# An attention and mixture-of-experts kernel: score and attention tiles of one PSUM bank, value columns in two parts, and the last gate logits summed ahead

## The chip, the cores and the metric

One Trainium2 chip, of which the kernel uses one core. A core has five engines, each with its own queue, worked off in order: TensorE (PE, matrix products; its weight loads are listed apart as PEld), VectorE (DVE), ScalarE (ACT), GpSimd (POOL) and SyncE (SP, which here only issues transfers). The 16 DMA engines move the data. PE writes its results to PSUM, eight banks of 512 floats on each of 128 partitions, and DVE and ACT read them there. Engines wait for each other on semaphores. The metric is the device time of one execution in microseconds (us); lower is better.

## What is computed

Causal attention with a window of 128 positions and a linear bias for each head, and behind it a mixture of experts in which every token goes to one expert, and every expert keeps at most 80 tokens, those of the largest gate weight. Batch 8, 8 heads, 576 positions, head size 64; 4608 tokens of 512 numbers; 8 experts with an inner size of 1024. All inputs are float32.

```python
scores = scale * np.matmul(q, k.transpose(0, 1, 3, 2))
bias = slopes[:, None, None] * (-np.abs(rel).astype(np.float32))[None, :, :]
mask = (rel >= 0) & (rel < window)
scores = np.where(mask, scores + bias[None], -1000000000.0)
attn = np.exp(scores - np.max(scores, axis=-1, keepdims=True))
attn = attn / (np.sum(attn, axis=-1, keepdims=True) + 1e-09)
x = np.matmul(attn, v)            # then tokens x 512
...
logits = x @ w_gate
expert_idx = np.argmax(logits, axis=1)
logits_shift = logits - logits.max(-1, keepdims=True)
probs = np.exp(logits_shift)
probs /= probs.sum(-1, keepdims=True) + 1e-09
gate_w = probs[np.arange(N), expert_idx]
...
for e in range(E):
    tok_idx = np.where(expert_idx == e)[0]
    if len(tok_idx) > capacity:
        tok_idx = tok_idx[np.argpartition(-gate_w[tok_idx], capacity)[:capacity]]
    h = np.maximum(x[tok_idx] @ w1[e], 0.0)
    out[tok_idx] = gate_w[tok_idx, None] * (h @ w2[e])
```

## The kernel before

**Recording.** The program isn't issued as it is written. A layer, `Plan`, records every instruction, orders them by its own table of costs and by the dependences between tiles, and then issues each engine's list. So nearly every row of the trace names line 352, where the layer issues, and rows are told apart by tiles. A dependence is kept per tile: an instruction that overwrites a tile waits for all that read the tile before.

**Units and steps.** The attention is cut into 144 units, 18 to a batch. A unit `i` is two halves (`hh` 0 and 1, the two heads that share a 128-row tile of `q` and `kp`). `scores(i)` makes four matmuls (the trace lists every float32 product of these kinds twice, so eight) into `sps[i % 2]`, a tile of two PSUM banks, a bank for each half; DVE adds the bias and takes the row's extremum (`e`, `mn`), POOL or ACT scales. `turned(i)` transposes `e` on PE into `pt`, ACT takes the exponential into `ptb`. `attend(i)` makes twelve matmuls (24 in the trace) of `ptb` with the values `v` into `avp`, again one tile of two banks, alternating between the halves in pairs. After every sixth unit `attended(n)` copies `av` to `xs` on ACT. The main loop runs over steps `c` of two units; nine steps `r` = 0 to 8 make a batch. At step `c` the scores of units 2c+4 and 2c+5 stand beside the attend of units 2c-2 and 2c-1.

**Gate logits and value columns.** The gate needs the logits of each attention output, which is a weighted sum of values. So the values are multiplied by the gate weights first: `value_logits(b)` multiplies the transposed values `l_vt` with `wg` (four groups by two banks, 16 in the trace) into the spare columns of a score tile, DVE or ACT adds a one and writes `lxb`; `value_columns(b)` transposes `lxb` back (five transposes, into both banks) and eight DVE copies lay the results into columns 64 to 72 of the value tile `v`. The attend matmuls then give output, logits and the sum of the exponentials together. For batch b+1 this stands at r = 3 and r = 8 of batch b; for batch 0 ahead of the loop, in the av banks, with copies aside into `xs`.

**Selection.** The choice of an expert and of the kept tokens of each batch (`merge_steps`) is spread over the steps of the batches behind it: `front` (norm, `gate`, parts) at r = 0 to 2, `turn` at 4, `diffs` at 5 to 7, `places` and `keep` at 0 and 1 of the next, `put_kept` at 2. For the last batch all of it stands behind the attention. There PE is kept busy with 100 small matmuls (`keep_clock`), which the layer places where PE would idle; ten larger ones (`warm_up`) stand ahead of the experts. Then tokens are gathered, eight experts are worked off, and the results are scattered.

**Transfers.** SP issues all loads and stores, in order, on eight rotating semaphores. `transfers(c)` names up to three for each step: the next batch's `l_vt`, `v`, `k`, `q`, the stores of the batch before (`store_x`). Where it has `None`, a filling transfer is taken from the list `fill` (pieces of the first two experts' weights, and zero writes of the output); what is left goes out behind the attention. At the start SP's order is: keys and queries of pair 0 in two pieces each, four `l_vt`, two small transfers of the gate weights (64x4x8), pair 1, four `v`, pairs 2 and 3.

## Time and profile before

| what | value |
|---|---|
| runs (us) | 338.27, 337.01, 338.03; median 338.03 |
| profiled execution (us) | 338.06 |
| its span (us) | 336.0 |
| mean granted clock of TensorE | 0.979 of full |
| PE, PEld busy | 92%, 67% |
| DVE, ACT, POOL busy | 56%, 43%, 39% |

The span is what the profiler sees from the first instruction to the last; the execution's own time is 2.06 us longer. All times of rows count from the start of the span. A row of a timeline gives start, duration, engine, line, operation, the tile written and the tile read, the shape and the count of merged instructions, and in brackets how long the engine had been idle and who released it. The granted clock is a share of the full 2.4 GHz.

### The profile page before, as it was taken

Reading aid. Unit: us, or ns where it says so; the run is one execution under the profiler, and the core shown is the slowest. Engines: PE = TensorE matmul, PEld = TensorE weight load, DVE = VectorE, ACT = ScalarE, POOL = GpSimd, SP = SyncE. Lnnn points to the kernel's source line nnn. Section 1 sums busy time; section 2 is a strip of 40 time slices with the busy share of each in tenths; the row PEclk is TensorE's granted clock in tenths of the full one; section 3 lists DMA queues with packets and bytes.
Section 4 is the critical chain, followed back from the end, with each engine's and each line's share of the span. In section 5 each row is a group of like instructions: output and inputs, shape, how many; then the busy total and the mean of one; then the engine's idle time right before and its main releaser. Section 6 shows DMA issues by size and latency. Waiting matters only on the chain. (4 is left out here: it accounts for less than half of the span.)

```text
span 336.0 us, 16380 instructions
## 1 busy us (share of the span) xinstructions
PE 309.5 (92%) x6722; PEld 223.8 (67%) x6722; DVE 188.2 (56%) x1017; ACT 145.1 (43%) x351; POOL 129.6 (39%) x350
## 2 busy tenths in 40 slices
PE   7897988989989989998998998999789999999993
PEld 6365755677777777776777777878585576655660
DVE  8854584787778678678678768777511011110100
ACT  1462664546555555454554554661213222233221
POOL 7443464428437336444644743830071111011111
PEclk9699999999999999999999999999789999999999
DMA  7969998899989998998998988778159999999930
GB/s 199 376 203 286 353 289 280 256 306 305 335 281 276 297 303 283 299 294 242 333 320 262 313 295 301 288 273 301 45 157 295 387 393 397 401 397 395 397 108 26
DMA packets 45530, 97.01 MB, mean 289 GB/s; under 512 B 5392, under 2 KB 5904, under 8 KB 45456
## 3 DMA queue, kind: packets, MB, share of 16 engines
q1 hardware_dynamic: 44432, 93.17, 81.4%
q0 software_dynamic: 1024, 2.81, 2.9%
q8 instruction: 53, 0.87, 1.2%
q14 instruction: 21, 0.17, 0.2%
HBM read 74.14 MB, written 21.81 MB: 286 GB/s over the span
## 5 line engine op out<-in xcount | busy, mean ns | idle before, releaser
L352 POOL TENSOR_SCALAR e<-e,mn 128x192 f32<-128x192 f32 (+1 forms) x216 | 88.7, 419 | 97.7 <-DVE mn L352 85.6
L352 ACT ACTIVATE ptb<-pt 128x256 f32<-128x256 f32 (+1 forms) x144 | 61.8, 463 | 58.3 <-PE pt L352 58.1
L352 PE MATMUL s<-kp,q 64*64 64x192 f32 (+1 forms) x1152 | 77.1, 319 | 10.3 <-DVE v L352 6.2
L352 PE MATMUL av<-v,ptb 64*64 64x73 f32 x3072 | 83.3, 228 | 2.4 <-issue 1.1
L352 PEld LDWEIGHTS av<-v,ptb 64*64 64x64 f32 x3072 | 71.2, 132 | 16.7 <-issue 12.1
L352 DVE CUSTOM_DVE_ANT_0 e<-s,bneg 128x192 f32<-128x192 f32 x192 | 60.6, 352 | 29.6 <-PE s L352 19.4
L352 PE MATMUL pt<-ident,e 128*128 128x128 f32 x400 | 60.6, 285 | 0.9 <-issue 0.4
L352 PEld LDWEIGHTS pt<-ident,e 128*128 128x128 f32 x400 | 43.2, 142 | 12.0 <-issue 4.4
L352 PEld LDWEIGHTS s<-kp,q 64*64 64x64 f32 x1152 | 36.7, 133 | 15.0 <-DVE v L352 7.2
L1297 DVE TENSOR_TENSOR ys<-ys,y 80x512 f32<-80x512 f32 x8 | 5.5, 683 | 73.4 <-ACT ys L1292 73.4
L352 ACT ACTIVATE e<-e,mn 128x192 f32<-128x192 f32 (+1 forms) x72 | 31.8, 441 | 31.9 <-DVE mn L352 31.9
L1290 PE MATMUL y<-w,hT 128*32 128x512 f32 (+1 forms) x288 | 42.8, 594 | 0.0
L1265 PEld LDWEIGHTS h<-xgTs,w 128*64 128x64 f32 x1024 | 35.9, 137 | 6.5 <-issue 6.0
L1265 PE MATMUL h<-xgTs,w 128*64 128x80 f32 x1024 | 37.2, 233 | 0.3 <-ACT xgTs L1224 0.3
L1241 POOL DMA_INDIRECT out_dram<-ys,sid x8 | 7.4, 922 | 72.0 <-ACT hT L1270 66.8
L352 ACT COPY xs<-av 128x438 f32<-128x438 f32 (+3 forms) x57 | 26.5, 509 | 14.4 <-PE av L352 13.5
L1290 PEld LDWEIGHTS y<-w,hT 128*32 128x32 f32 (+1 forms) x288 | 10.5, 105 | 25.0 <-issue 24.2
L352 DVE TENSOR_SCALAR_CACHE_REDUCE ncm<-s 128x272 bf16<-128x272 f32 (+8 forms) x69 | 22.7, 380 | 2.1 <-ACT ncm L352 1.6
L352 DVE DVE_READ_ACCUMULATOR2_ANT mn<- 128x1 f32 x288 | 23.8, 83 | 0.0
L352 DVE CUSTOM_DVE_ANT_0 e<-s,bn 128x128 f32<-128x128 f32 x64 | 16.0, 288 | 9.8 <-PE s L352 6.9
L1270 ACT ACTIVATE hT<-h 128x320 f32<-128x320 f32 x16 | 7.0, 437 | 29.1 <-PE h L1265 29.1
L352 DVE CUSTOM_DVE_ANT_0 e<-s,bnx 128x192 f32<-128x192 f32 x32 | 10.2, 355 | 16.3 <-PE s L352 16.2
(147 smaller groups left out, 326.9 us busy)
## 6 DMA issues: line engine op xcount, KB each, us to landing
w<-in_moe_w_dram SPq DMA_DIRECT2D x48, 512.0 KB, 11.1
v<-in_v_dram SPq DMA_DIRECT2D x32, 328.5 KB, 5.0
x_dram<-xs SPq DMA_DIRECT2D x32, 292.0 KB, 4.7
l_vt<-in_vt_dram SPq DMA_DIRECT2D x32, 288.0 KB, 4.4
out_dram<-zero SPq DMA_DIRECT2D x36, 256.0 KB, 3.8
kp<-in_k_dram SPq DMA_DIRECT2D x31, 288.0 KB, 4.9
q<-in_q_dram SPq DMA_DIRECT2D x31, 288.0 KB, 4.5
w<-in_moe_w_dram SPq DMA_DIRECT2D x32, 256.0 KB, 4.5
```

The costliest lines, as they stand in the source:

```text
L352: c.ins = c.f(*c.args, **c.kw)
L1241: put = nc.gpsimd.indirect_dma_start(out=out, out_offset=bass.IndirectOffsetOnAxis(ap=sid[:, e:e + 1], axis=0), in_=ys, in_offset=None, bo ...
L1265: nc.tensor.matmul(hp[64 * hh:64 * hh + 64, R * fi:R * fi + R], lhsT=a[:, cc, f0:f0 + 64], rhs=xgT[:, cc], start=(cc == 0), stop=(cc == NC ...
L1270: relu = nc.scalar.activation(hT[:, 4 * f2:4 * f2 + 4].rearrange("p c r -> p (c r)"), hp[:, 0:4 * R], AF.Relu)
L1290: nc.tensor.matmul(o, lhsT=hT[:, f_, l0:l1], rhs=c[:, f_], start=st, stop=sp)
L1297: nc.vector.tensor_tensor(ys, ys, yp[0:R, 0:DM], ALU.add)
```

## The change

A tile for each PSUM bank: `sps` is two by two tiles and `avp` two, so each wait is for one bank. `attended` copies by half, so the copies at n = 1 are six instead of three; in the last batch the second half of the last copy is on DVE. `value_columns` works in two parts: units 0 to 2 into the first bank at r = 8, with four copies, and units 3 and 4 into the second bank at r = 2 of the batch itself, with four copies. For batch 0 the logits of groups 0 and 1 come first, with copies straight from `av`; groups 2 and 3 follow at c = 1 and 2, and the logits of batch 1 move from r = 3 to r = 6. The gate weights come as one transfer of 128x128, laid out on the host. The last batch's logits are summed in three parts (`logit_sum`), two of them in the loop. A few copies of the selection go to ACT, the last batch's stores of units 3 and 4 are issued earlier, and `transfers` has four `None` instead of six a batch.

```diff
-    sps = [psum.tile([P, 2, 512], F32, name=f"s{i}") for i in range(2)]
-    avp = psum.tile([P, 2, 512], F32, name="av")
+    sps = [[psum.tile([P, 512], F32, name=f"s{i}_{k}") for k in range(2)] for i in range(2)]
+    avp = [psum.tile([P, 512], F32, name=f"av{k}") for k in range(2)]
...
     load_pair(0, 0)
-    for g in range(NP):
+    wg = const.tile([P, NP, 32], F32, name="wg")
+    nc.sync.dma_start(out=wg.rearrange("p g c -> p (g c)"), in_=w_gate)
+    for g in range(2):
         load_vt(0, g)
-    wg = const.tile([P, NP, 32], F32, name="wg")
-    nc.gpsimd.memset(wg, 0.0)
-    for hh in range(2):
-        nc.sync.dma_start(
-            out=wg[64 * hh:64 * hh + 64, :, 9 * hh:9 * hh + 8],
-            in_=w_gate.rearrange("(g hh p) e -> hh p g e", g=NP, hh=2)[hh],
-        )
     load_pair(0, 1)
-    for g in range(NP):
+    for g in range(2):
         load_v(0, g)
+    for g in range(2, NP):
+        load_vt(0, g)
     load_pair(0, 2)
     load_pair(0, 3)
+    for g in range(2, NP):
+        load_v(0, g)
...
-        nc.vector.tensor_copy(ttt[b % 2][:, S:S + R], kp[0:KS, 0:R])
+        (nc.scalar.copy if b == LAST else nc.vector.tensor_copy)(ttt[b % 2][:, S:S + R], kp[0:KS, 0:R])
...
+    def lay(b, bank, gs, us, hh, par):
+        rows, of = (LOW, HIGH)[hh], (LOW, HIGH)[par]
+        u0, u1 = us
+        lv = bank[:, 0:32 * (gs[1] - gs[0]) * (u1 - u0)].rearrange("p (u g c) -> p g u c", u=u1 - u0, c=32)
+        k1 = min(2 * u1, NKB)
+        nc.vector.tensor_copy(
+            vts[b % 2][rows, gs[0]:gs[1], 2 * u0 + par:k1:2, D:VW],
+            lv[of, :, 0:(k1 - 2 * u0 - par + 1) // 2, 9 * hh:9 * hh + 9])
+
+    def value_columns(b, bank, us, gs=(0, NP)):
+        lx, ch = lxs[b], slice(32 * gs[0], 32 * gs[1])
+        n = ch.stop - ch.start
         with nc.together():
...
+        for hh in range(2):
+            for par in range(2):
+                lay(b, bank, gs, us, hh, par)
...
     def attended(n):
...
+        for hh in range(2):
+            copy = nc.vector.tensor_copy if hh and b == LAST and n == 2 else nc.scalar.copy
+            av = avp[hh][:, 0:6 * VW].rearrange("p (s c) -> p s c", c=VW)
+            if n == 1:
+                copy(xs[:, 3].rearrange("p (g h) c -> p h g c", h=2)[:, hh], av[:, 0:4])
+                for j, rows in ((0, LOW), (1, HIGH)):
+                    copy(
+                        xs[0:64, 4].rearrange("p (u j h) c -> p j h u c", u=2, j=2)[:, j, hh], av[rows, 4:6])
...
+    def logit_sum(b, n=None):
+        whole_, first, last = (0, NU, 0, H), n == 0, n == 2
+        u0, u1, h0, h1 = {None: whole_, 0: (0, 3, 0, 4), 1: (3, NU, 0, H), 2: (0, 3, 4, H)}[n]
+        U, N = u1 - u0, h1 - h0
+        ve = nc.vector if last else nc.gpsimd
...
+        ve.tensor_tensor(
+            lw, xs[:, :, :, D:VW - 1], xs[:, :, :, VW - 1:VW].broadcast_to([P, U, N, E]), ALU.mult)
+        to = small.tile([P, U, E], F32, tag="lg2", name=f"lg2_{b}", bufs=1) if last else lg
+        nc.vector.tensor_reduce(to, lw.rearrange("p u h e -> p u e h"), axis=AX.X, op=ALU.add)
+        if last:
+            nc.vector.tensor_tensor(lg, lg, to, ALU.add)
...
-        if b < LAST and r == 3:
+        if b < LAST and r == (3 if b else 6):
             yield value_logits(b + 1, two, add_ones)
         if b < LAST and r == 8:
-            yield value_columns(b + 1, two)
+            yield value_columns(b + 1, two[0], (0, 3))
+        if b and r == 2:
+            yield value_columns(b, two[1], (3, NU))
+        if c == 1:
+            yield value_logits(0, two, add_ones, (2, NP))
+        if c == 2:
+            yield value_columns(0, two[0], (0, NU), (2, NP))
...
-            3: v_[3:4] + x_[1:2] + [None],
+            3: v_[3:4] + x_[1:2],
...
-            7: kq(3) + [None],
+            7: kq(3),
             8: vt_[0:1] + [None, None],
         }[r]
-        if b == 0 and r < 4:
-            at_ = [[], vt_[0:2], vt_[2:4] + v_[0:1], v_[1:4]][r]
+        if b == 0 and r < 8:
+            at_ = {
+                2: vt_[0:1], 3: vt_[1:4], 4: kq(0) + v_[0:1], 5: v_[1:4], 6: kq(1) + kq(2)[0:1],
+                7: kq(2)[1:2] + kq(3),
+            }.get(r, [])
...
-    whole(value_logits(0, (avp[:, 0], avp[:, 1]), add_ones_act))
+    whole(value_logits(0, avp, add_ones_act, (0, 2)))
     make_bias(1)
     scored(3)
+    whole(value_columns(0, avp[0], (0, NU), (0, 2)))
     strict(turned, 2)
     scored(4)
-    whole(value_columns(0, (avp[:, 0], avp[:, 1]), xsb[1].rearrange("p u h c -> p (u h c)")[:, 0:NU * P]))
...
+        if b == LAST and r in (3, 6):
+            logit_sum(b, r // 3 - 1)
...
-    while fill:
+    for _ in range(8):
         fill.pop(0)()
     keep_clock(nc.last, 100)
...
-    for u in range(NU):
+    for u in range(3):
         store_x(LAST, u)
+    while fill:
+        fill.pop(0)()
```

The order of the instructions shows the places where this acts. The first is PE at step r = 8 of batch 2, where the value columns of batch 3 are made (`lxb_317` of before is `lxb_320` of the changed kernel; brackets name the engines and transfer queues that an instruction waits for). Before:

```order
L352 MATMUL av_83<-v0_94,ptb51_342 64x73 x6
L352 MATMUL s1_82<-kp1_91,q3_1_331 64x128 [waits DMAHW2_49,DMAHW1_49,DVE_49]
L352 MATMUL s1_82<-kp1_91,q3_1_331 64x128 x3
L352 MATMUL s1_82<-ident_102,lxb_317 128x128 x4
L352 MATMUL s1_82<-ident_102,lxb_317 64x128
```

The same place of the changed kernel:

```order
L352 MATMUL s1_0_83<-kp1_94,q3_1_334 64x128 [waits DMAHW7_49,DMAHW0_49,DVE_49]
L352 MATMUL s1_0_83<-kp1_94,q3_1_334 64x128
L352 MATMUL s1_1_84<-kp1_94,q3_1_334 64x128 [waits DVE_49]
L352 MATMUL s1_1_84<-kp1_94,q3_1_334 64x128
L352 MATMUL s1_0_83<-ident_105,lxb_320 128x128 x3
```

The first bank takes three transposes, and the second half of the scores has a wait of its own; the other two transposes stand some 125 rows later, at r = 2 of batch 3.

The second place is ACT at the end of a batch's second group, n = 1, in batch 1. Before:

```order
L352 ACTIVATE ptb31_258<-pt1_80 128x384 [waits PE_49,Activation_49]
L352 COPY xs1_123<-av_83 128x2x4x73 [waits PE_49]
L352 COPY xs1_123<-av_83 64x2x2x73 x2
L352 ACTIVATE e35_262<-e35_262,mn35_263 128x3x64 [waits DVE_49,Activation_49,Pool_49]
L352 ACTIVATE ptb32_264<-pt0_79 128x384 [waits PE_49,Activation_49]
```

The same in batch 3 of the changed kernel:

```order
L352 ACTIVATE ptb67_415<-pt1_80 128x384 [waits PE_49,Activation_49]
L352 COPY xs1_126<-av0_85 128x4x73 [waits DMAHW1_49,PE_49]
L352 COPY xs1_126<-av0_85 64x2x73 [waits DMAHW4_49]
L352 COPY xs1_126<-av0_85 64x2x73
L352 COPY xs1_126<-av1_86 128x4x73 [waits PE_49]
L352 COPY xs1_126<-av1_86 64x2x73 x2
L352 ACTIVATE e71_419<-e71_419,mn71_420 128x3x64 [waits DVE_49,Activation_49,Pool_49]
```

Three copies of both banks became three of the first bank and three of the second.

The third place is DVE at the start, where the reduction of unit 3 (`e3`) and the columns of batch 0 stand. Before:

```order
L352 SCALAR_TENSOR_TENSOR bnx_89<-rp_86 64x192 x4
L352 CAST pf_159<-pi_158 128x1 [waits Pool_49]
...
L352 CAST ita_120<-ij_164 80x640 [waits Pool_49]
L352 ISA e3_137,mn3_138<-s1_82,bn0_88 128x2x64 [waits PE_49]
...
L352 COPY xs1_123<-av_83 128x128 [waits Activation_49]
L352 COPY xs1_123<-av_83 64x128
L352 COPY v0_94<-xs1_123 64x2x5x9 [waits DMAHW5_49,DMAHW4_49,DVE_49]
```

The changed kernel:

```order
L352 SCALAR_TENSOR_TENSOR bnx_92<-rp_89 64x192 x3
L352 ISA e3_140,mn3_141<-s1_0_83,bn0_91 128x2x64 [waits DVE_49,PE_49]
...
L352 TENSOR_SCALAR ts0_109<-pf_162 128x5 [waits DVE_49]
L352 ISA e4_143,mn4_144<-s0_0_81,bneg_90 128x3x64 [waits PE_49]
...
L352 COPY v0_97<-av0_85 64x2x5x9 [waits DMAHW1_49,DMAHW2_49,PE_49,Activation_49]
L352 COPY v0_97<-av0_85 64x2x4x9
```

The reduction of unit 3 moved ahead of the constants, and the copies aside are gone.

## Rows read from the trace of the kernel before

**Rows 1.** The page, busy time, share of the span and instructions of each engine.
```profile
PE 309.5 (92%) x6722; PEld 223.8 (67%) x6722; DVE 188.2 (56%) x1017; ACT 145.1 (43%) x351; POOL 129.6 (39%) x350
```

**Rows 2.** Busy time by stretch: length, PE, PEld, DVE, ACT, POOL, clock, DMA share, GB/s.
```profile
8.00:15.00 7.00, 5.78 (x40) 2.60 (x40) 6.04 (x36) 2.79 (x7) 3.38 (x14) 0.51 1.04 364
...
20.00:34.40 14.40, 12.15 (x336) 8.87 (x328) 6.01 (x36) 6.39 (x16) 5.06 (x13) 1.00 0.89 277
...
116.30:143.30 27.00, 25.69 (x648) 19.77 (x642) 20.68 (x120) 14.25 (x36) 13.63 (x36) 1.00 0.92 298
...
236.40:248.30 11.90, 8.73 (x66) 7.21 (x64) 5.12 (x24) 1.74 (x7) 4.54 (x6) 0.71 0.17 44
248.30:326.60 78.30, 78.30 (x1404) 48.62 (x1408) 9.23 (x14) 22.26 (x45) 10.32 (x12) 1.00 0.96 349
```

**Rows 3.** Waits of PE, 36 to 222 us: total, times, longest.
```profile
PE s L352 <- DVE v L352: 6.2, 7, 0.9
```

**Rows 4.** Timeline, r = 8 of batch 3, all engines.
```profile
123.08 2.02 DVE L352 COPY v<-s 64x108 f32<-64x108 f32 x8
...
123.71 0.56 PE L352 MATMUL av<-v,ptb 64*64 64x73 f32 x24
124.34 0.95 ACT L352 COPY xs<-av 128x438 f32<-128x438 f32 x2 [0.44 <-PE av L352]
...
125.15 0.56 PE L352 MATMUL s<-kp,q 64*64 64x192 f32 x8 [0.88 <-DVE v L352]
```

**Rows 5.** Timeline, r = 2 of batch 4, PE and, apart, DVE.
```profile
133.02 0.51 PE L352 MATMUL s<-kp,q 64*64 64x192 f32 x8
...
135.40 0.36 DVE L352 CUSTOM_DVE_ANT_0 e<-s,bnx 128x192 f32<-128x192 f32 x1 [1.17 <-PE s L352]
```

**Rows 6.** Timeline, n = 1 copies of batch 4, all engines.
```profile
143.34 1.35 ACT L352 COPY xs<-av 128x584 f32<-128x584 f32 x3 [1.07 <-PE av L352]
...
143.94 0.77 PE L352 MATMUL pt<-ident,e 128*128 128x128 f32 x5
...
144.75 0.26 PEld L352 LDWEIGHTS av<-v,ptb 64*64 64x64 f32 x9 [0.28 <-ACT xs L352]
```

**Rows 7.** Groups of ACT by shape: count, busy, mean ns, idle before.
```profile
L352 ACT COPY xs<-av 64x292 f32<-64x292 f32 x16 | 6.4, 399 | 0.1
...
L352 ACT COPY xs<-av 128x584 f32<-128x584 f32 x8 | 5.2, 651 | 5.9 <-PE av L352 5.9
```

**Rows 8.** Groups of DVE by shape, the value columns' copies.
```profile
L352 DVE COPY v<-s 64x108 f32<-64x108 f32 x28 | 7.5, 268 | 0.3
...
L352 DVE COPY v<-s 64x72 f32<-64x72 f32 x14 | 3.2, 225 | 0.2
...
L352 DVE COPY v<-s 64x36 f32<-64x36 f32 x14 | 2.8, 198 | 0.2
```

**Rows 9.** Timeline, the start.
```profile
10.78 2.15 PE L352 MATMUL av<-l_vt,wg 128*32 128x288 f32 x16 [0.88 <-DMA wg<-in_moe_w_gate_dram]
...
13.63 0.29 DVE L352 CUSTOM_DVE_ANT_0 e<-s,bn 128x128 f32<-128x128 f32 x1
...
17.14 0.47 PE L352 MATMUL av<-v,ptb 64*64 64x73 f32 x7 [0.66 <-ACT v L352]
...
26.54 1.16 PE L352 MATMUL s<-l_vt,wg 128*32 128x288 f32 x10 [1.66 <-DMA l_vt<-in_vt_dram]
...
29.43 0.56 PE L352 MATMUL s<-kp,q 64*64 64x192 f32 x8 [0.59 <-DVE lxb L352]
```

**Rows 10.** Timeline, behind the attention.
```profile
228.76 0.56 DVE L352 TENSOR_TENSOR ob<-tt,itb 128x400 bf16<-128x400 f32 x1
...
231.00 3.97 PE L352 MATMUL pt<-identb 128*128 128x128 bf16 x68
...
232.50 0.20 DVE L352 TENSOR_REDUCE mx<-lg 128x5 f32<-128x40 f32 x1
...
237.75 0.31 DVE L352 TENSOR_SCALAR_CACHE_REDUCE ncm<-s 128x144 bf16<-128x144 f32 x1 [1.60 <-ACT ncm L352]
```

More of the change, by code (lines that the diff above doesn't have):

```diff
@@ L811, in gate @@
         ve = nc.vector if b in FAST else nc.gpsimd
[L812 to L817 removed]
+        if b < LAST:
+            logit_sum(b)
+        lg = sums[b]
         mx = small.tile([P, NU], F32, tag="mx", name=f"mx{b}")
```

110 lines of the change are left out of this document (46 added, 64 removed).

## The prediction

> **What bounds the kernel now.** I read the page's busy shares first, then the table of busy time by stretch, the waits of PE, and the timelines around each wait. PE is busy 309.5 of 336.0 us and no other engine comes near [rows 1], so an edit is worth what it gives back to PE: idle time of PE, or time in which its clock is low. By stretch [rows 2]: a batch in the middle (116.3 to 143.3 us, one of seven periods alike) has 25.69 us of PE work in 27.0, so 1.3 us are idle. The stretch of the experts, 248.3 to 326.6, is PE without a gap at the full clock; the change leaves its instructions as they are, so nothing is won there. Two stretches show the granted clock at or near the lower of its two levels, 1.2 GHz for 2.4: 8 to 15 us (0.51) and, in part, 236.4 to 248.3 (0.71). Both are chains of waits, as is the first attention up to 34.4 us, with 12.15 us of PE work in 14.4.
>
> The idle time of the batches has one main name: over 36 to 222 us PE waits 7 times, 6.2 us in all, for DVE's copies of the value columns [rows 3]. The profiled execution took 338.06 us, 2.06 more than its span; the median of the three runs is 338.03, so the sum below is made against 338.06 and needs no correction.
>
> **The change part by part.**
>
> *Value columns in two parts, banks apart (batches 1 to 7).* Before, five transposes fill both banks of one score tile and eight copies empty them: DVE is on them from 123.08 to 125.10, while PE, done with its av matmuls at 123.71 + 0.56 = 124.27, waits until 125.15 to write the next scores there, 0.88 idle [rows 4]. Now three transposes go into the first bank at this place, with four copies, and the other two with four smaller copies follow some three steps later, in the second bank. Four large copies of 268 ns overlap: eight took 2.02, or 0.25 each, so I count 1.05. Begun at 123.08 they end at 124.13, and 0.14 before PE wants the bank. The second bank is free from the start. So the wait goes: 7 x 0.88 = **-6.2**. It is a tight cover: if the four start 0.35 later, 7 x 0.2 = 1.4 comes back.
>
> The second part lands where DVE has idle time: soon after the third step's small copies it waits 1.17 us for PE [rows 5], and the four copies are two of 225 and two of 198 ns [rows 8], some 0.75 overlapped. They stand ahead of a score reduction that feeds PE through POOL and ACT, so I charge 0.1 a batch, **+0.7** in 7 batches; bounds 0 (the idle time takes all) and 0.4 each, half of the 0.75.
>
> *Copies by half after attention.* At the end of a batch's second group ACT makes three copies in 1.35 us, and PE, after its transposes, waits 0.28 to overwrite av [rows 6]. Now there are six. The short form costs 399 ns at 292 elements and the long one 651 at 584 [rows 7], so 0.86 ns an element and some 0.15 fixed; a copy of 128x292 is 0.40, of 64x146 0.27, six together 2 x 0.40 + 4 x 0.27 = 1.88, less five overlaps of 0.05 (three rows summing to 1.45 took 1.35) = 1.63. The second bank is thus free 0.28 later than now, and PE, whose attend matmuls alternate between banks in pairs, gets only two matmuls ahead. 8 x 0.28 = **+2.2**, the 8 from [rows 7]; bounds 0 (ACT starts on the first bank earlier and PE's transposes last longer) and +3.5 (0.44 each). The other copies keep their number and now wait for one bank each: nothing.
>
> A rule of the Trainium skill (Perfetto Trace Analysis, Optimizing Scalar/DVE Operations) speaks against the split: every ScalarE or VectorE instruction has a fixed cost, put at about 51 ns for ScalarE on PSUM, and grouping pays if the engine is saturated. By that figure three more copies are 0.15 us, an estimate, 1.2 in 8 batches, and the sum below would end 1.0 lower. The fixed part read from the rows is about three times as large, and the rows decide here.
>
> *The waits themselves.* A tile per bank gives each unit's second half of scores a semaphore wait of its own: the order shows 113 more waits among PE's score groups and 20 more among its attends. A group that has such a wait and finds it satisfied starts without a gap: the scores at 133.02 have no idle time in front [rows 5]. I take 0; the upper bound is a rival below.
>
> Steady part: -6.2 + 0.5 + 2.2, **-3.3**; bounds -6.2 and, with every upper end, +1.5.
>
> *The start.* PE waits until 10.78 for the second of two small gate transfers that stand behind four value loads; its 16 logit matmuls then take 2.15 at half clock, and the chain runs over scores (DVE at 13.63), ACT's copies aside, and copies back, to the first attend at 17.14, itself 0.66 late [rows 9]. Now the gate weights are one transfer ahead of the value loads, groups 0 and 1 alone (8 matmuls, half of 2.15) go first, and DVE copies straight from PSUM; in DVE's order the reduction of unit 3 moves from behind fourteen small constants to ahead of them. 0.88 + 1.07 = 1.95 less before unit 3: the first attend at about 15.2, **-1.9**. Bounds -0.9 (only the wait for the gate weights goes, DVE holds the rest) and -2.5.
> The other half of the logits comes back behind it: 8 matmuls at the full clock and five transposes, 0.95 us of PE (16 in 2.15 at half clock make 8 in 0.54 at the full one; five transposes of twice the columns took 0.77 [rows 6], so 0.4): **+0.95**.
> Batch 1's logits: before, PE stood 1.66 for a value transfer and 0.59 for what DVE made of it [rows 9]. The change moves these logits three steps later, behind transfers that are issued only a step later: 2.25 go, and ten matmuls that took 1.16 run at the pace of data already there, some 0.5 less: **-2.7**, bounds -1.7 (the DVE wait stays) and -2.8. New waits for eight more DVE instructions among the first units, 0.1 each at half of them: **+0.45**, bounds 0 and 1.5.
> The new order of transfers brings pair 1 of keys and queries forward and costs 48 KB more of gate weights, 0.2 us of the transfers' time at 224 GB/s or more [rows 2], ahead of nothing that is late now. Start: **-3.2**, bounds -0.2 and -4.4.
>
> *The tail.* Before, DVE reaches the maximum of the last logits at 232.50, after a product and a sum over 320 elements; most of that is now made two steps ahead, and only 96 elements are left, behind DVE's own copy of the second half of av. From the end of ob, 228.76 + 0.56 = 229.32, I count that copy at 0.55, as ACT's (two in 0.95 [rows 4]) and a little more, and five short operations at 0.2 to 0.25 each (the maximum over 40 elements takes 0.20 [rows 10]): the maximum at about 231.0, 1.5 earlier. The sums ahead run on POOL and DVE in the last batch, where both have idle time. But PE's filler (68 matmuls, 3.97 from 231.00 [rows 10]) stands in the queue before the next transposes; 58 of them take 3.39 and end 0.58 earlier. So PE's queue is next late: **-0.6**. Then DVE's first reduction of the pairwise comparison, which waited 1.60 until ACT had done another bank at 237.75 [rows 10], waits only for PE, 0.65 earlier: **-0.65**, bounds 0 (ACT's part ends last) and -0.7. Two more small norms fall among DVE's work for batch 6: **+0.15**.
> Tail: **-1.1**, bounds 0 and -1.5.
>
> *Transfers.* The filling ones are only spread otherwise, in SP's queue as before; the last weights are needed after 248.3. Eight of the zero writes stay ahead of the stores of x and three go behind. Cost nothing where the cover is the 0.17 DMA share of 236.4 to 248.3 [rows 2]; without it, 3 x 256 KB at the 349 GB/s of the next row is 2.2 us more before the gathers.
>
> Sum: -3.3 - 3.2 - 1.1 = -7.6, so 338.06 - 7.6 = 330.46, **330.5 us**.
>
> **The rivals.**
> *A second stall in the place of the first.* The four copies come late, the six copies cost their upper bound and the second part its own: 1.4 + 1.3 + 2.1 = 4.8 of the gain is lost, 335.3. For it speaks the cover of only 0.14; against it that the score reduction which now stands ahead reads the second bank first. With half of it, 332.9.
> *More than counted.* The split copies cost nothing, since PE goes on with the first bank, and the start reaches its bound: -5.5 - 4.4 - 1.1 = -11.0, thus 327.1.
> *The start gives nothing.* DMA share is 0.89 from 20 to 34.4 us [rows 2], and batch 1's keys are now issued behind hoisted zero writes; a stall like the old one, 1.66 and 0.59, returns at keys and queries, and the start is worth -0.95: 332.7.
> *The waits cost (the other side).* Each of the 133 additional waits of PE delays the queue. From 57 ns each (7.6 / 133), about one filler matmul (3.97 / 68 = 58), the whole gain is gone; at 80 ns the time is 341.1. Against it stands the gapless row at 133.02; for it only that no row of before has two such waits within one unit's scores.
> *The change does not do what it says*: the copies still block both banks. The order speaks against it, since each bank has its own wait.
>
> **How the numbers follow.** The forecast with its own range 328.5 to 332.5: 0.53. A second stall: 0.15. More than counted: 0.12. The start gives nothing: 0.10. The waits cost: 0.06. No effect of the banks: 0.04. The range 326.5 to 335.5 holds the first four but for the ends of the second and third. Half a per cent, 1.7 us, is about what a measurement of this kernel can tell from no change, so faster is under 336.4: the first four cases, some of the last two; 0.88. Within: 0.07. Slower: 0.05.
>
> **What would show it.** Right: no PE wait for DVE's value copies at the last step of a batch; PE's wait for ACT before the third group's attend grown from 0.28 to about 0.56; periods of batches near 26.5; the first attend near 15.2; no wait for the value transfer of batch 1; the maximum near 231.0 less what was gained ahead of it, with the filler ending last; DVE's comparison released by PE. Wrong: idle time of 0.05 or more in front of the second half of many score groups, a new DVE wait in each batch's third step, or PE idle after 20 us for keys.

## The result

The changed kernel took 333.5 us, the median of four runs (332.67 to 338.03), beside 338.1 us for the kernel before (337.01 to 338.27). The ratio is 0.9862, with a 95% interval of 0.9828 to 0.9897: 1.4% faster, 4.6 us of the 7.6 that the prediction counted. Medians in this document are over all executions, ratios leave those out that the chip disturbed, and since the profiles of after_again, slots_again, shift_128, same_again and warm_15 are of such executions, the sizes of their waits are told but no cause rests on them.

The profiled execution took 333.14 us with a span of 331.4. From its page: span, busy time by engine, TensorE's granted clock in 40 slices (tenths, 9 is 90% or more), and the queue that carries instructions (packets, MB, share).

```profile
span 331.4 us, 16415 instructions
...
PE 308.1 (93%) x6727; PEld 224.7 (68%) x6727; DVE 192.4 (58%) x1026; ACT 146.5 (44%) x372; POOL 129.8 (39%) x351
...
PEclk9999999999999999999999999999779999999998
...
q8 instruction: 53, 0.87, 1.0%
```

PE is busy 1.4 us less than in [rows 1] and the span is 4.6 shorter, so 3.2 us of the gain is idle time that went. Where, three stretches tell, cut at ACT's n = 1 copies of batch 0 and of batch 7 and at the first expert's products (length, then busy time of PE, PEld, DVE, ACT, POOL, clock, DMA share, GB/s). Changed kernel:

```profile
30.95:217.53 186.58, 178.46 (x4467) 137.21 (x4459) 144.49 (x815) 102.80 (x274) 94.17 (x254) 1.00 0.92 305
217.53:241.59 24.06, 20.86 (x347) 17.70 (x339) 14.61 (x73) 7.55 (x25) 6.22 (x10) 0.93 0.46 154
241.59:331.40 89.81, 83.62 (x1436) 51.15 (x1436) 9.78 (x15) 23.98 (x48) 11.27 (x13) 0.96 0.84 308
```

The same stretches of the kernel before:

```profile
34.40:222.53 188.13, 177.58 (x4450) 136.09 (x4443) 141.50 (x812) 100.20 (x252) 95.32 (x255) 1.00 0.91 297
222.53:248.29 25.76, 22.14 (x347) 18.59 (x339) 14.46 (x73) 7.28 (x20) 5.79 (x9) 0.87 0.49 167
248.29:336.00 87.71, 81.97 (x1436) 49.49 (x1436) 9.92 (x15) 24.01 (x48) 11.29 (x13) 1.00 0.87 316
```

So the start gave 34.40 - 30.95 = 3.45, the seven periods 188.13 - 186.58 = 1.55, the tail 25.76 - 24.06 = 1.70, and the experts took 89.81 - 87.71 = 2.10 back. 3.45 + 1.55 + 1.70 - 2.10 = 4.60, the difference of the spans.

**The periods.** Waits of PE in the first of these stretches of the changed kernel (total, times, longest; waits under 0.15 us aren't counted):

```profile
PE s L352 <- issue: 4.5, 8, 1.1
PE av L352 <- issue: 2.1, 5, 0.6
PE av L352 <- ACT xs L352: 0.7, 4, 0.2
PE pt L352 <- issue: 0.4, 1, 0.4
```

DVE's value copies are gone from the list: 6.2 us in seven waits [rows 3]. ACT costs 0.7, after 0.5. New is the sum of the waits put down to "issue", in which PE waits for nothing that the profile shows: 7.0 us here, 3.5 in the kernel before over its stretch. -6.2 + 3.5 + 0.2 = -2.5 of idle time, and PE's busy time grew by 178.46 - 177.58 = 0.88.

How the first wait went, in the timeline around r = 8 of the changed kernel (start, length, what, and in brackets the idle time before and its releaser; DVE, then PE):

```profile
118.51 1.11 DVE L352 COPY v<-s 64x108 f32<-64x108 f32 x4
...
118.73 0.61 PE L352 MATMUL av<-v,ptb 64*64 64x73 f32 x24
119.16 0.50 PE L352 MATMUL s<-kp,q 64*64 64x192 f32 x8
```

Four copies where [rows 4] has eight, 1.11 us (1.05 counted), and the scores behind start with no idle time before them. At the end of a batch's second group, ACT and then PE (here batch 7):

```profile
217.53 1.75 ACT L352 COPY xs<-av 128x292 f32<-128x292 f32 x6 [0.46 <-PE av L352]
...
218.82 0.34 PE L352 MATMUL av<-v,ptb 64*64 64x73 f32 x4
219.32 0.70 PEld L352 LDWEIGHTS av<-v,ptb 64*64 64x64 f32 x32 [0.32 <-ACT xs L352]
219.33 0.85 PE L352 MATMUL av<-v,ptb 64*64 64x73 f32 x32 [0.17 <-ACT xs L352]
```

The wait of 0.28 in [rows 6] is one of the weight loads (PEld). The matmuls, from which PE's idle time is counted, start there in the kernel before with no idle time of their own (under 0.08 us in seven of the eight batches, 0.45 in the first):

```profile
144.75 0.36 PE L352 MATMUL av<-v,ptb 64*64 64x73 f32 x8
```

The six copies take 1.75 us, 0.12 more than counted. Like beside like, the weight loads wait 0.32 us for 0.28, and the matmuls 0.08 to 0.17 in the seven batches where they waited under 0.08: PE has the first bank early, four matmuls go into it, and the second is nearly free by then.

**The start.** PE:

```profile
9.30 1.16 PE L352 MATMUL av<-l_vt,wg 128*32 128x288 f32 x8
...
14.47 0.36 PE L352 MATMUL av<-v,ptb 64*64 64x73 f32 x8 [0.93 <-DVE v L352]
...
15.91 1.16 PE L352 MATMUL s<-l_vt,wg 128*32 128x288 f32 x8
...
30.43 0.48 PE L352 MATMUL av<-v,ptb 64*64 64x73 f32 x16 [1.44 <-issue]
31.17 1.18 PE L352 MATMUL s<-l_vt,wg 128*32 128x288 f32 x16
```

The first attend begins at 14.47 for 17.14, and no wait for a value transfer is left [rows 9]. But eight logit matmuls of two groups last 1.16 us, as long as sixteen of four groups (1.18).

**Behind the attention.** PE's filler, DVE's maximum and first comparison, the first expert's transposes and products:

```profile
225.72 3.41 PE L352 MATMUL pt<-identb 128*128 128x128 bf16 x58
...
226.42 0.20 DVE L352 TENSOR_REDUCE mx<-lg 128x5 f32<-128x40 f32 x1
...
231.25 0.31 DVE L352 TENSOR_SCALAR_CACHE_REDUCE ncm<-s 128x144 bf16<-128x144 f32 x1 [0.94 <-PE s L352]
...
240.76 0.50 PE L1251 MATMUL xgT<-ident,xn 80*128 80x80 f32 x4 [1.25 <-issue]
241.59 6.29 PE L1293 MATMUL h<-xgTs,w 128*64 128x80 f32 x128 [0.33 <-ACT xgTs L1252]
```

The comparison waits for PE and no longer for ACT, as counted against [rows 10]. The loss is the last line: the same products took 4.65 us before. Their clock, by the microsecond:

```profile
241.00:242.00 1.00, 0.67 (x16) 0.51 (x16) 0.75 (x1) 0.49 (x2) 0.69 (x2) 1.00 0.59 178
...
243.00:244.00 1.00, 1.00 (x20) 1.00 (x18) 0.00 (x0) 0.00 (x0) 0.77 (x1) 0.50 1.02 375
...
245.00:246.00 1.00, 1.00 (x20) 1.00 (x18) 0.00 (x0) 0.44 (x1) 0.69 (x2) 0.50 1.04 373
```

From 243 to 246 the clock is at 1.2 GHz, half of 2.4.

### The profile page after: what moved, and what is told of

The parts are those of the page before. It is cut to its first block, busy times and chain, and to the rows that moved or that the text cites. A ratio compares the mean times of both kernels' runs of the same rounds, so it can differ in the third digit from the quotient of the medians.

```text
span 331.4 us, 16415 instructions
## 1 busy us (share of the span) xinstructions
PE 308.1 (93%) x6727; PEld 224.7 (68%) x6727; DVE 192.4 (58%) x1026; ACT 146.5 (44%) x372; POOL 129.8 (39%) x351
## 5 line engine op out<-in xcount | busy, mean ns | idle before, releaser
L352 PE MATMUL av<-v,ptb 64*64 64x73 f32 x3072 | 87.3, 228 | 5.6 <-issue 3.5
L352 PEld LDWEIGHTS av<-v,ptb 64*64 64x64 f32 x3072 | 73.4, 132 | 22.1 <-issue 16.7
L352 PE MATMUL s<-kp,q 64*64 64x192 f32 (+1 forms) x1152 | 79.4, 314 | 3.7 <-issue 2.0
L352 DVE CUSTOM_DVE_ANT_0 e<-s,bneg 128x192 f32<-128x192 f32 x192 | 62.2, 352 | 31.5 <-PE s L352 26.9
L352 PE MATMUL pt<-ident,e 128*128 128x128 f32 x400 | 59.3, 281 | 1.5 <-ACT e L352 1.0
L352 PEld LDWEIGHTS s<-kp,q 64*64 64x64 f32 x1152 | 39.9, 132 | 5.1 <-issue 2.7
L1293 PEld LDWEIGHTS h<-xgTs,w 128*64 128x64 f32 x1024 | 37.5, 142 | 6.4 <-issue 6.0
L1293 PE MATMUL h<-xgTs,w 128*64 128x80 f32 x1024 | 38.8, 239 | 0.3 <-ACT xgTs L1252 0.3
L352 ACT COPY xs<-av 128x438 f32<-128x438 f32 (+2 forms) x79 | 28.4, 401 | 14.7 <-PE av L352 13.8
L1318 PE MATMUL yx_d<-w,hT 128*32 128x512 f32 x32 | 15.2, 598 | 0.0
## 6 DMA issues: line engine op xcount, KB each, us to landing
v<-in_v_dram SPq DMA_DIRECT2D x32, 328.5 KB, 5.4
```

What stands on the lines that cost most here:

```text
L352: c.ins = c.f(*c.args, **c.kw)
L1293: nc.tensor.matmul(hp[64 * hh:64 * hh + 64, R * fi:R * fi + R], lhsT=a[:, cc, f0:f0 + 64], rhs=xgT[:, cc], start=(cc == 0), stop=(cc == NC ...
L1318: nc.tensor.matmul(o, lhsT=hT[:, f_, l0:l1], rhs=c[:, f_], start=st, stop=sp)
```

## What the issue waits are

In all these traces PE's instructions arrive during the run: 53 pieces, 0.87 MB (the last line of the page above), 16 KB each. Counting PE's weight loads, matmuls and semaphore instructions in order of their starts, the issue waits stand at one place in each 256, whatever operation is there. From the packet records of the changed kernel, worked out for six of them:

```
piece  begins   lasts   PE's late instruction   gap    gap ends after the piece landed (us)
  2     28.10   0.93      961 =  3*256 + 193    1.66    1.40 us
  6     49.95   0.95     1985 =  7*256 + 193    1.10    1.27
  9     66.69   0.94     2753 = 10*256 + 193    1.38    1.46
 11     77.28   0.95     3265 = 12*256 + 193    0.66    1.44
 19    119.20   0.94     5313 = 20*256 + 193    0.88    1.42
 20    124.89   1.04     5569 = 21*256 + 193    0.85    1.32
```

The gap here is the time between two starts; the idle time of the rows is shorter, since the matmul before still runs. The second of them in the views: the instruction queue's line of 49.9 to 51.0 us, and the PE line of the wait. From 45.9 to 49.9 the same view has nothing on that queue, and data at 297 GB/s on the others.

```profile
q8 instruction: 1, 0.02, 5.4%
```
```profile
52.17 0.33 PE L352 MATMUL s<-identb,ts 128*64 128x128 bf16 x3 [0.88 <-issue]
```

PE had passed the same place of the 256 before, 1729 = 6*256 + 193, at 45.95, and this transfer began 4.00 us later. Counted so, a piece's delay is the time from that place to the start of the transfer. PE needs some 5.3 us for 256 instructions here (187 us for 35 pieces), and some 0.95 of transfer and 1.4 behind it stand in all six lines, so a piece that begins more than about 2.95 us late stops PE, an estimate from these numbers. The median delay of the pieces 2 to 36 is 1.63 us in the kernel before and 3.16 in the changed one. The Trainium skill (Trainium Architecture — The Big Picture, The software stack) has the instruction streams copied to the engines when the program is loaded. The trace differs, with its 53 pieces between 16 and 319 us.

For the lost part of the gain one theory and its rivals follow. Supply: the pieces stand behind data in the transfer engines, and the changed kernel moves more data while attention runs; take data away and the waits go. The rivals: the waits are those of the new semaphores, or of one execution; or PE, no longer held by DVE, comes to the next piece sooner. A question apart is the clock, at the start and in the first expert.

## The experiments

Twelve runs on three more chips, each chip with its own runs of the kernel before; the runs of one chip are compared.

| run | chip | median, us | of before, us | ratio | 95% interval |
|---|---|---|---|---|---|
| same_again | 2 | 340.04 | 342.45 | 0.9999 | 0.9935 to 1.0063 |
| warm_15 | 2 | 341.01 | 342.45 | 1.0033 | 0.9971 to 1.0096 |
| logits_whole | 2 | 338.41 | 342.45 | 0.9932 | 0.9864 to 1.0000 |
| columns_at_once | 2 | 341.62 | 342.45 | 1.0125 | 0.9967 to 1.0282 |
| before_again | 3 | 343.06 | 342.92 | 1.0030 | 0.9977 to 1.0084 |
| no_zero_writes | 3 | 331.46 | 342.92 | 0.9698 | 0.9606 to 0.9790 |
| shift_128 | 3 | 344.37 | 342.92 | 1.0028 | 0.9978 to 1.0077 |
| slots_as_before | 3 | 337.15 | 342.92 | 0.9862 | 0.9745 to 0.9978 |
| after_again | 4 | 332.98 | 337.22 | 0.9858 | 0.9803 to 0.9912 |
| slots_again | 4 | 331.12 | 337.22 | 0.9848 | 0.9810 to 0.9885 |
| zeros_behind | 4 | 330.31 | 337.22 | 0.9813 | 0.9771 to 0.9856 |
| slots_zeros_whole | 4 | 330.46 | 337.22 | 0.9848 | 0.9794 to 0.9902 |

**The changed kernel again (same_again, after_again).** No edit.

> The changed kernel once more, unchanged, as the reference of this set. Both theories: 333.1 us, 0.986 of the kernel before; first products of the first expert start near 241.6 us and take 6.3 us where the kernel before has 4.65; PE stands 6 to 8 us in all without a wait that the profile names (issue).

> The changed kernel once more, as the mark for the three runs beside it on this chip. Supply theory (PE's instructions come in 53 pieces of 16 KB that stand behind the data in the transfer engines; a piece that comes late stops PE): the idle before PE put down to issue between 30 and 222 us sums to 8 to 12 us, each wait over 0.4 us ends about 1.4 us after a piece landed, and the time is 0.983 to 0.990 of the kernel before, 333.5 us on a chip that runs the kernel before at 338. Chance theory (the waits of the profiled run were that run's own): the sum falls to the 3 to 5 us of the kernel before.

Chip 4 repeats the result, 0.9858, with 10.2 us of issue waits in the seven periods. On chip 2 the gain isn't there, 0.9999: the kernel before takes 336.5 to 346.7 us there, and in the changed one's trace the issue waits of the seven periods come to 11.5 us, and others break up the first expert's products (below). So the gain is not the same on every chip; why is open.

**The kernel before again (before_again).** No edit.

> The kernel before, unchanged, for a trace on the same chip as the three that follow. Theory A (PE takes its instructions in pieces of 256, each fetched by a transfer of 16 KB behind the data already queued, and stands still where the piece isn't there): the waits of PE without a name stand each at a multiple of 256 instructions from the others, and sum to about 5 us between 30 and 222 us, some 7 less than in the changed kernel. Rival B (they are gaps of the record or chance): they stand anywhere and differ from one execution to the next.

The wait for DVE stands as in [rows 3], and issue is 3.6 us over its seven periods; with 1.29 ahead of them, at 31.75, that is the 5 us expected, each at the same place in its 256. What the pair of traces in the result hid is at the start. PE:

```profile
10.11 1.18 PE L352 MATMUL av<-l_vt,wg 128*32 128x288 f32 x16 [1.11 <-DMA wg<-in_moe_w_gate_dram]
...
15.11 0.65 PE L352 MATMUL av<-v,ptb 64*64 64x73 f32 x8 [0.17 <-ACT ptb L352]
```

The same kernel without the half clock of 8 to 15 us (1.00 here, 0.51 in [rows 2]): the logits take 1.18 us, not 2.15, and the first attend is at 15.11, not 17.14. ACT's copies of the first two groups, before_again:

```profile
21.34 0.95 ACT L352 COPY xs<-av 128x438 f32<-128x438 f32 x2 [0.39 <-PE av L352]
...
32.71 1.35 ACT L352 COPY xs<-av 128x584 f32<-128x584 f32 x3 [2.23 <-PE av L352]
```

The changed kernel has them at 22.14 and 30.95. At the full clock the edits at the start are thus worth 32.71 - 30.95 = 1.8 us, not 3.45: the first attend 0.64 earlier, the first copies 0.8 later, and all of the gain behind them, at batch 1's logits. (Each has one issue wait ahead of that place, 1.29 and 1.44 us.) The other 1.7 goes with the clock of one execution, as far as a profile of another chip can tell. Nor did the change remove that: over 8 to 15 us the clock is 0.51 to 0.52 in two of thirteen profiles (before, logits_whole), 0.76 in two (warm_15, slots_again) and 0.93 or more in nine; shift_128, whose start differs, isn't among them.

**The first logits in one piece (logits_whole).** All four groups of batch 0 at once, and the value transfers in the old order:

```diff
-    for g in range(2):
+    for g in range(NP):
         load_vt(0, g)
...
-    for g in range(2, NP):
-        load_vt(0, g)
...
-        if c == 1:
-            yield value_logits(0, two, add_ones, (2, NP))
...
-    whole(value_logits(0, avp, add_ones_act, (0, 2)))
+    whole(value_logits(0, avp, add_ones_act))
```

> The gate logits of batch 0 in one piece again, all four groups ahead of the loop, their four value loads in front of pair 1; the columns stay in halves. Theory A (matmuls of the four groups overlap, so 16 take the 1.18 us that 8 take, and the second half is paid for twice): PE has 1.16 us less behind the first attend, the copies after unit 5 and all that follows come 1.0 to 1.2 earlier, 332.0. Rival B (the start is bound by transfers: two value loads of 288 KB more ahead of pair 1 take 1.5 us at 380 GB/s): the first attend moves from 14.5 to 15.5 or more, and the time stays within 0.5 of 333.1.

```profile
10.22 2.15 PE L352 MATMUL av<-l_vt,wg 128*32 128x288 f32 x16
...
16.33 0.36 PE L352 MATMUL av<-v,ptb 64*64 64x73 f32 x8 [0.32 <-DVE v L352]
```

Its profile has the half clock at the start, and at this clock the first attend is 0.81 before [rows 9], with the rest of the change at the start: the logits begin at 10.22 for 10.78, and DVE copies straight from `av`. Its first copies stand at 22.96, only 0.82 behind the changed kernel's though the first attend is 1.86 behind: undivided, there is no second 1.16 to pay. The time, 0.9932 beside 0.9999 on its chip, doesn't separate the two.

**Both parts of the columns at r = 8 (columns_at_once).** The tiles stay one to a bank:

```diff
-        if b and r == 2:
-            yield value_columns(b, two[1], (3, NU))
+            yield value_columns(b + 1, two[1], (3, NU))
```

> The value columns of batches 1 to 7 all at the last step again, five transposes and eight copies in a row, each bank still a tile of its own. Theory A (PE's gain from the second part is eaten by its own instruction supply: where it no longer waits for DVE it runs out of instructions): 7 waits for the copies come back, 0.3 to 0.9 each, 3 to 6 us in all, but PE's time without a named wait falls from some 7 us to 4 in 31 to 217 us, so the kernel is only 1 to 2.5 us slower, 334 to 335.6. Rival B (the rest of the steady part's loss is the copies by half and the later columns): the waits without a name stay, and the kernel is 4 to 6 us slower, 337 to 339.

PE's waits from batch 0's to batch 7's copies:

```profile
PE s L352 <- DVE v L352: 2.8, 8, 0.4
PE s L352 <- issue: 2.6, 2, 1.4
```

So of 6.2 us of waits the banks alone take 3.4, and dividing the columns the other 2.8. But theory A holds here: with the 2.8 us for DVE back, issue is 3.5 us, and the seven periods take 186.7 us, where logits_whole, with the columns in parts on the same chip, has 8.0 us of issue and 188.1. In these two profiles what dividing the columns gave is taken again by late instructions. The times, 1.0125 with an interval from 0.9967, can't tell the theories apart.

**Longer warm-up for the experts (warm_15).** `warm_up(10)` before the experts becomes `warm_up(15)`.

> Fifteen matmuls instead of ten between the selection and the first expert. Theory A (PE idles 1.25 us there while the gathers run, and the clock falls for the first expert because of that idle time): the idle time shrinks below 0.7, the first expert's products take 4.65 again for 6.3, the kernel gets 1.6 us faster, 331.5. Rival B (the clock falls there because of the earlier pause of 1.33 us before the last placement, or by chance): the products stay at 6.3, the time stays at 333.1 or grows by the 0.9 that five more matmuls last.

```profile
249.06 0.47 PE L1251 MATMUL xgT<-ident,xn 80*128 80x80 f32 x4 [0.21 <-issue]
249.90 1.60 PE L1293 MATMUL h<-xgTs,w 128*64 128x80 f32 x38 [0.36 <-issue]
```

The idle time before the transposes goes from 1.25 to 0.21 us, but the time doesn't fall (1.0033 beside 0.9999). On chips 2 and 3 issue waits break the first expert's products in the kernels looked at, the one before too, and from its first product to the next transposes it is 9.9 to 11.6 us where the other chips have 4.6 to 7.2; this run can't tell what holds the clock there. Nor does the length of the pause order the others: zeros_behind has 2.84 us of it and 5.68 us from product to transposes, the kernel before 0.71 and 4.57, the changed one 1.25 and 6.22.

**Without the zero writes (no_zero_writes).** 35 of the 36 transfers that zero the output are left out, 9.2 MB; the rows that no token is kept for stay unwritten.

```diff
     for c in range(NTOK // P):
-        fill.append(lambda c=c: nc.sync.dma_start(out=out[P * c:P * (c + 1)], in_=zero[:, 0:DM]))
+        if c == 0:
+            fill.append(lambda c=c: nc.sync.dma_start(out=out[P * c:P * (c + 1)], in_=zero[:, 0:DM]))
```

> The changed kernel without 35 of the 36 zero writes of the output (9.2 MB less; rows of tokens that no expert keeps are left unwritten). Theory A (instruction pieces wait behind queued data): the delay from the point where a piece is asked for to the start of its transfer falls below 2.5 us from 3.2, the waits without a name between 30 and 222 us fall from 8 or more to under 4 us, and the kernel is 4 to 6 us faster than the changed one. Rival B (the pieces come late for a reason of their own, a fixed latency): the waits stay at 8 or more and the time within 1 us.

```profile
PE s L352 <- issue: 2.7, 3, 1.7
...
PE av L352 <- issue: 0.5, 1, 0.5
```

331.46 us, a ratio of 0.9698; the interval ends at 0.9790, below those of the changed kernel on the first and the fourth chip. On this chip the changed kernel itself has no run; slots_as_before, which differs by two slots a batch, took 334.9 to 339.6 us there, with 6.2 us of issue; all four executions without the writes, 330.6 to 333.9 us, lie below that. Issue is 3.2 us where the result's profile has 7.0, all of it before 78 us; the median delay is 1.81, and the three periods from batch 2's copies to batch 5's take 25.3 to 25.4 us each instead of 26.6 to 27.7. PE's matmuls and the waits of each bank's own tile are those of the changed kernel, and PE gets through its periods sooner, so neither those waits nor PE's pace alone is what stops it.

**Other places in the stream (shift_128).** The matmuls at the program's start become 4 of 128 and 38 of 16 columns, so that each later instruction stands elsewhere in its 256:

```diff
-    def warm_up(n):
+    def warm_up(n, w=P):
...
-            nc.tensor.matmul(wp[:, 0:P], lhsT=z, rhs=z, start=True, stop=True)
+            nc.tensor.matmul(wp[:, 0:w], lhsT=z, rhs=z[:, 0:w], start=True, stop=True)
...
-    warm_up(10)
+    warm_up(4)
+    warm_up(38, 16)
```

> The changed kernel with 128 more PE instructions at the very start (4 matmuls of 128 columns and 38 of 16 for 10 of 128, in the same time), so that every boundary of 256 instructions falls half a piece earlier in the program. Theory A: the waits without a name move to other matmuls, 128 instructions earlier or half a piece apart, still at multiples of 256; their sum stays between 5 and 12. Rival B (they belong to certain matmuls of the program): they stay at the matmuls where they are.

The waits moved to other operations (45.06, 66.28, 128.92, 133.85, 175.22 us), at the same place in each 256, and the instruction queue carries 54 pieces instead of 53. The time says nothing: narrow matmuls last as long as wide ones, some 0.2 us a row with their weights, so the start is longer, and the first copies come 11.9 us later.

**The filling slots back (slots_as_before, slots_again).** The same kernel on two chips:

```diff
-            3: v_[3:4] + x_[1:2],
+            3: v_[3:4] + x_[1:2] + [None],
...
-            7: kq(3),
+            7: kq(3) + [None],
```

> The changed kernel with the two slots for filling transfers that the change takes out of each batch put back (r = 3 and r = 7). Theory A, in the form that denser transfers of the change make the pieces late: the waits without a name change by more than 2 us, down if the longer list of slots spreads the transfers, and the time with them. Rival B (the pieces are late because PE comes to the boundary sooner, whatever the slots): the waits stay within 2 us of the changed kernel's, the time within 1.

> The changed kernel with the two filling slots a batch that it dropped (r=3 and r=7) put back, so that the same 36 zero writes are spread over more places. Supply theory, if the places of the zero writes matter: idle put down to issue 5 to 7 us between 30 and 222 us where the changed kernel beside it has 8 to 12, and 1.5 to 3 us less time than that kernel. Rival (places don't matter, only the amount of data that moves during attention does): same time as the changed kernel beside it within 0.5%, idle put down to issue within 2 us of it.

On chip 4 the time is no different from the changed kernel's, 0.9848 beside 0.9858, with 8.7 and 10.2 us of issue; on chip 3, with 0.9862 and 6.2 us, no run of the changed kernel stands beside it. In the time no run shows an effect of the slots.

**Twelve zero writes held back (zeros_behind).**

```diff
-                q = fill.pop(0) if fill and c > 4 else None
+                q = fill.pop(0) if len(fill) > 12 and c > 4 else None
...
-    for _ in range(8):
+    while len(fill) > 12:
         fill.pop(0)()
...
     for u in range(3):
-        store_x(LAST, u)
+        lead = store_x(LAST, u)
     while fill:
-        fill.pop(0)()
+        nc.pace(fill.pop(0)(), lead)
```

> The changed kernel with 12 of the 36 zero writes (3.1 MB of 9.4) held back behind the last batch's stores, where its trace moves almost nothing between 230 and 239 us. Supply theory: a third of what leaving out 35 of them gave (issue waits 3.2 us in place of 8 to 12, and some 8 to 10 us of time), so 2.5 to 3.5 us less than the changed kernel beside it, all of it before 222 us; the gathers of the first experts still start within 0.5 us of where they did after the last store. Rival (they meet the gathers and the first weights there): the first expert's products start 1 to 3 us later after the last store, and the time is the same within 0.5%. Rival (it was the waits on value columns' chain, not the data): no batch is shorter, 0.

SP's queue, then PE's waits over the seven periods, then the stretch from 226 us (columns as in the result):

```profile
224.14 7.67 SPq L352 DMA_DIRECT2D out_dram<-zero  x12
```
```profile
PE s L352 <- issue: 2.2, 3, 1.5
...
PE av L352 <- issue: 0.7, 2, 0.4
```
```profile
226.00:230.00 4.00, 2.56 (x41) 2.18 (x39) 3.02 (x17) 0.65 (x3) 0.44 (x2) 0.96 1.02 377
```

Issue falls to 2.9 us, none of it behind 80 us, and the four periods from batch 2's copies to batch 6's take 25.4 to 25.7 us. Batch 7's copies stand at 211.77, 5.76 us ahead of the result's profile. But the first expert begins at 237.59, 25.82 behind them where it began 24.06 behind: the first gather is issued as long behind the copies as in the changed kernel (19.03 us for 19.04), but the writes now stand ahead of its data, PE waits 2.84 us before the transposes, and 1.76 us is given back, so on this the rival was right. Its time, 0.9813, is 0.45% or 1.5 us below after_again's 0.9858: the right sign, smaller than expected, and the intervals overlap.

**Slots, held writes and whole logits together (slots_zeros_whole).** The edits of the three kernels above.

> Three of the pieces together: the changed kernel with the slots at r=3 and r=7 back, 12 zero writes held behind the last stores, and the first batch's logits in one piece. Supply theory: idle put down to issue 3 to 6 us between 30 and 222 us; against the changed kernel beside it -2.5 to -3.5 us for the writes held back, 0 to -2 for the slots, 0 to -1 for the logits (the halves last 1.16 us each where the whole lasts 1.18): 3 to 6 us less. Rival (what is given in one place is taken in another, since PE then waits for the same transfers at other matmuls): within 0.5% of the run with the writes alone.

0.9848: issue 3.4 us, batch 0's n = 1 copies at 29.54, and the first expert's products 1.5 us slower than in zeros_behind (7.23 to the next transposes, 5.68 there). The 3 to 6 us expected aren't there, and of the kernels that do all the work none is shown to beat the changed one on its chip.

**What the profiles say together.** For each run, the data started on all queues and PE's idle time put down to issue, from batch 0's n = 1 copies to batch 7's (seven periods), and in the four of them from batch 1's copies to batch 5's, with the zero writes that SP issued there:

| run | seven: MB | issue, us | four: MB | zero writes | issue, us | length, us |
|---|---|---|---|---|---|---|
| no_zero_writes | 50.97 | 3.2 | 29.35 | 0 | 0.5 | 102.6 |
| zeros_behind | 53.82 | 2.9 | 30.74 | 4 | 0.7 | 103.5 |
| slots_zeros_whole | 55.89 | 3.4 | 31.46 | 0 | 1.8 | 104.2 |
| before_again | 55.42 | 3.6 | 31.48 | 1 | 0.4 | 107.6 |
| before | 55.81 | 3.5 | 31.52 | 1 | 0.6 | 107.5 |
| slots_as_before | 57.24 | 6.2 | 32.62 | 5 | 2.8 | 105.7 |
| logits_whole | 56.98 | 8.0 | 33.44 | 16 | 5.0 | 109.5 |
| after | 56.85 | 7.0 | 33.94 | 16 | 5.1 | 109.2 |
| columns_at_once | 56.14 | 3.5 | 34.00 | 16 | 1.8 | 108.3 |

Over the seven periods the changed kernel issues 32 pieces of weights, 26 key loads and 25 zero writes, the kernel before 31, 25 and 24: 0.8 MB. What moved is their place. In the four periods the changed kernel, and then the kernel before, issued (count, KB each, median us to landing):

```profile
out_dram<-zero SPq DMA_DIRECT2D x16, 256.0 KB, 5.0
w<-in_moe_w_dram SPq DMA_DIRECT2D x16, 256.0 KB, 5.2
```
```profile
w<-in_moe_w_dram SPq DMA_DIRECT2D x24, 256.0 KB, 4.3
out_dram<-zero SPq DMA_DIRECT2D x1, 256.0 KB, 6.0
```

Eight pieces of weights went out of these periods with the two slots a batch, and 16 zero writes stand in their room; with the slots back (slots_as_before) it is 24 and 5. In the last two periods it is the other way, 23 zero writes before and 8 now. So the four periods are 1.7 us longer than before, although 3.5 us of waits for DVE went from them, and the gain of the steady part lies in the other three.

zeros_behind takes 12 of the 16 writes out of the four periods, and they have 0.7 us of issue and last 103.5 us, on another chip than the 5.1 and 109.2 of the changed kernel. Whether the writes delay PE's pieces by their amount alone or also by their kind is not shown. And columns_at_once has as many writes there but 1.8 us of issue, beside 1.5 us of waits for DVE: how soon PE comes to the next piece counts too.

## Why the prediction was right, and where it was not

The range of 326.5 to 335.5 and the sign held, and 333.1 stands 2.7 above the 330.5 forecast, outside the forecast's own 328.5 to 332.5. It lies near the figures of two rivals, 332.7 and 332.9, but neither happened: no stall at keys and queries took the start's gain, and the waits for the value columns did not come back. What took 3.5 us in the seven periods was in no step and no rival, so that the range held is in part luck. By its steps:

- **Value columns, -6.2: right.** The seven waits went in full, with 1.11 us for the four copies where 1.05 were counted. columns_at_once divides it: 3.4 for the banks, 2.8 for the parts. The second part, +0.7, stands against 0.88 more busy time of PE, but the same matmuls have 176.0 us of it in no_zero_writes and 176.5 in zeros_behind, less than the 177.6 of the kernel before, so the 0.88 isn't the columns'.
- **Six copies, +2.2: mis-sized.** ACT's length was near (1.75 for 1.63), but PE's wait grew by 0.2 us in all. The step read a wait of the weight loads as one of PE and carried ACT's extra time over to PE whole; the first bank, free early, hides most of it. Three more copies cost 0.40 us of ACT's time, 0.13 each, near the 0.15 that the rows gave. The Trainium skill (Perfetto Trace Analysis, Optimizing Scalar/DVE Operations) puts the fixed cost at about 51 ns, which makes 0.15 us for the three, an estimate. The trace has more than twice that.
- **The waits themselves, 0: right.** Of the 1008 rows of score matmuls in the seven periods five have idle time of 0.05 us or more in front, and no_zero_writes, with the same waits, has middle periods of 25.35 us. The rival that ended on the other side falls.
- **Transfers, nothing: the step that failed.** It took the filling transfers to be "only spread otherwise", asked who waits for their data, and left out that PE's own instructions come by transfers too. Spread otherwise, 16 zero writes stand in the four periods where one stood, and issue costs 3.5 us more in the seven, with 1.44 at 30.43 in the start. Nor did three zero writes go behind: all were issued by 224 us.
- **The start, -3.2: right in sum and wrong in its parts.** 3.45 were measured, some 1.7 of it, by before_again, the half clock of the one execution that the sum was made against; that the sum came out is luck. First attend 2.67 earlier, 0.64 at the full clock; the second half of the logits +1.16 for their matmuls alone where 0.54 stood, since half the groups take as long as all; batch 1's logits the rest, and there the wait for the transfer and the wait for DVE both went.
- **The tail, -1.1: right in kind, too small.** 1.70 were measured, beyond its bound of 1.5 (1.40 against before_again), with the filler 0.56 shorter and DVE's comparison released by PE. From batch 7's copies the maximum comes 8.89 us on where it was 9.97, 1.1 earlier for 1.5 counted; the filler begins at 8.19 for 8.47, and the comparison at 13.72 for 15.22.
- **The experts, 0: wrong.** The same instructions took 2.1 us more, 1.64 of it the first products, in part at half the clock. What the clock does to a stretch that is left alone was not asked. after_again on another chip has it too (6.29 us again); before_again, on a chip that breaks these products up, can't be set beside it. What drew the clock down is open: the pause before it grew from 0.71 to 1.25 us, the run meant to tell that apart couldn't, and zeros_behind, with a pause of 2.84, was quicker.

Against the forecast in the periods: -6.2 + 0.2 + 3.5 + 0.9 = -1.6, where -3.3 stood. (The prediction's line for the steady part writes 0.5 where its own step has 0.7; its sum is made with 0.7.)

## What to carry to other kernels

Where transfers fill most of the time, as here (a DMA share of 0.92), an engine with thousands of small instructions has one more transfer to wait for, its own code. An edit that speeds the engine up, or pushes transfers into a stretch that is full, is paid for there: look for waits put down to issue that stand at one place in each 256 instructions. Count background transfers by stretch and not over the whole: here their sum hardly changed, and their place did. A sum made against one profiled execution takes over that execution's clock; read the same stretch in a second one before a gain is put down to an edit. And a copy that is split between two banks costs the engine that waits only what the second bank is late, not what the copies last.

## What was unexpected in the hardware

- PE's instructions come in pieces of 16 KB, 256 instructions, during the run, some 0.95 us each, and where a piece began late, PE stood until 1.3 to 1.5 us after it landed (six of six worked out).
- Matmuls of 128*32 weights in two groups of columns last as long as those in four: eight 1.16 us, sixteen 1.18.
- The clock of one and the same stretch, 8 to 15 us, was 0.51 in one execution of the kernel before and 1.00 in another.
- Chips differ in what they show of one kernel: over the first expert's products, the kernel before took 4.57 us on one and 11.02 on another, there with six issue waits some 0.7 us apart.
